# Merging the half-array attention visits of groups two to four in a planned attention-and-feed-forward kernel

## The chip, the cores and the metric

One Trainium2 chip, one of its cores. The metric is the device time of one execution in microseconds; several runs are given by their median. TensorE is called PE, VectorE DVE, ScalarE ACT, GpSimd POOL and SyncE SP, which issues the transfers.

## The reference

Attention with 4 batches, 8 heads, 768 positions and a head size of 64, each position looking at 8 global keys and the last 96 local ones, with a linear bias by distance; its output, as 3072 rows of 512, goes through a feed-forward layer of 2048 channels. All weights of that layer are stored in 64 bits.

```python
def _attn_ref(q, k, v, n_global, n_local):
    scores = scale * np.matmul(q, k.transpose(0, 1, 3, 2))
    ...
    scores = np.where(keep, scores + bias, -1000000000.0)
    scores = scores - np.max(scores, axis=-1, keepdims=True)
    a = np.exp(scores)
    a = a / (np.sum(a, axis=-1, keepdims=True) + 1e-09)
    return np.matmul(a, v).astype(np.float32)

def _moe_ref(x, w_in, w_out):
    h = x @ w_in
    g = np.where(h > 0.0, h, alpha * (np.exp(np.minimum(h, 0.0)) - 1.0))
    return (g @ w_out).astype(np.float32)
```

## The kernel before

The 3072 rows are worked in 12 groups of 256 rows (two q tiles of 128 rows), three groups to a batch. Of each group the attention of 8 heads is computed first, in four pairs of heads (`pair`), and gives the tile `x`, kept as a rounded high part `xh` and a rest `xl`. Then 16 chunks of the feed-forward layer follow (`moe`): for each chunk `up` computes `h` in 12 matmuls of 256 columns, ACT and DVE turn it into `gh` and `gl` (high part and rest), and `down` adds 6 matmuls of 512 columns to the sums `o0` and `o1`. The first three groups share their chunks in turns (five chunks of each, then five, then six), since the weights are still being made in that time: `weight` loads a chunk's 64-bit words (`bits`), and ACT and DVE make 32-bit numbers of them in tile `g`: an absolute value on ACT, a clamp, a shift and two merges on DVE, a rounding on ACT (`w`, high part) and a subtraction on DVE (`w`, rest). There are 32 such weights.

The first four groups use the route `heads32`: plain 32-bit matmuls for the scores and the values. The two heads of a pair lie on 64 partitions each, so the scores (tile `s`, from `rk` and `rqv`) use half of TensorE's rows for each head, and the values (tile `pv`, from `pt` and `rqv`) half of its columns for each head. Between them stand, for each q tile and head, a reduction on DVE that adds the mask table and finds the maximum (`pr`, `nmax`), an exponential on ACT, a scaling, a transpose on TensorE (tile `t`, all rows and columns) and a copy to `pt`. Each q tile is one call of `heads32`: one visit to the half rows for its scores, one to the half columns for its values. The scores of a visit take two banks, one a head.

The order of the instructions is not the order of the code. `Plan.add` collects operations with the engines that may do them, an estimated duration and a due time; `Plan.order` then places them one by one, on the engine that can start earliest, the earliest due first, with tiles taken from named slots (`SLOTS`; for the first groups other slots too, from `EARLY`, which lend places of weights not yet loaded). What reaches each engine is a fixed list. Where the plan sees PE unoccupied before the first `h`, `warm` puts matmuls on a tile of ones into the list (`none<-fill`, 512 columns each), which compute nothing that is used. An operation that the plan marks as using the port that DVE and POOL share is kept apart from another such operation.

## Time and profile before

| what | us |
|---|---|
| median of 3 runs (lowest, highest) | 722.8 (722.57, 723.8) |
| the profiled execution, whole | 722.63 |
| its span in the profile | 720.8 |
| PE busy in it | 703.1 |
| DVE busy | 520.9 |
| ACT busy | 510.4 |
| POOL busy | 202.2 |

The span begins with the first instruction and ends with the last; 1.8 us of the profiled execution lie outside it. PE's matmuls are pipelined and their ends are modelled: a record says how long one matmul was under way, not how much time it took from the engine. Here the time that work takes on PE is therefore read from start to start: the start of the next row less the start of this one. A row of the timeline merges like instructions that follow one another; an x4 of a 32-bit matmul with half rows or half columns stands for two matmuls of two passes each.

### The profile page before, as it was taken

Reading aid. Unit: us, or ns where it says so; the run is one execution under the profiler, and the core shown is the slowest. Engines: PE = TensorE matmul, PEld = TensorE weight load, DVE = VectorE, ACT = ScalarE, POOL = GpSimd, SP = SyncE. Lnnn points to the kernel's source line nnn. Section 1 sums busy time; section 2 is a strip of 40 time slices with the busy share of each in tenths; the row PEclk is TensorE's granted clock in tenths of the full one; section 3 lists DMA queues with packets and bytes.
Section 4 is the critical chain, followed back from the end, with each engine's and each line's share of the span. In section 5 each row is a group of like instructions: output and inputs, shape, how many; then the busy total and the mean of one; then the engine's idle time right before and its main releaser. Section 6 shows DMA issues by size and latency. Waiting matters only on the chain.

```text
span 720.8 us, 13887 instructions
## 1 busy us (share of the span) xinstructions
PE 703.1 (98%) x4716; PEld 616.4 (86%) x4716; DVE 520.9 (72%) x1570; ACT 510.4 (71%) x1467; POOL 202.2 (28%) x264
## 2 busy tenths in 40 slices
PE   8999999999999999999999999999999999999996
PEld 5676788888889899889899899898899899999895
DVE  5998899996448876876786786885886787685210
ACT  5897988866557877867776777776776776876442
POOL 1000000000004442533434443343344344332221
PEclk9999999999999999999999999999999999999999
DMA  7623790001113222131231322312321331210001
GB/s 297 240 68 90 301 414 18 23 1 46 53 59 111 76 83 82 54 105 57 78 103 38 99 55 80 104 54 68 97 76 54 91 96 53 82 54 1 30 1 35
DMA packets 22256, 63.50 MB, mean 88 GB/s; under 512 B 2721, under 2 KB 4769, under 8 KB 22177
## 3 DMA queue, kind: packets, MB, share of 16 engines
q1 hardware_dynamic: 22176, 62.53, 25.8%
q8 instruction: 39, 0.64, 0.4%
q14 instruction: 41, 0.33, 0.1%
HBM read 56.23 MB, written 6.29 MB: 87 GB/s over the span
## 4 chain that ended last, share of the span: by engine, by line
PE 81%; DVE 9%; ACT 4%; issue 3%; DMA 1%; SPq 0%; POOL 0%; ACTq 0%; DVEq 0%; POOLq 0%
PE h L597 32%; PE o L619 31%; PE pv L578 3%; PE t L566 3%; PE s L552 3%; PE pv L533 2%; PE s L510 2%; PE t L523 2%; DVE pr L467 2%; DVE ks L292 1%; DMA rqv<-in_qkv_dram 1%; PE none L743 1%; DVE pr L477 1%; DVE e L605 1%; ACT pr L479 1%
## 5 line engine op out<-in xcount | busy, mean ns | idle before, releaser
L597 PE MATMUL h<-xh,w 128*128 128x256 f32 x1536 | 248.2, 284 | 0.0
L597 PEld LDWEIGHTS h<-xh,w 128*128 128x128 f32 x1536 | 225.9, 189 | 24.5 <-issue 1.7
L619 PE MATMUL o<-w,gh 128*128 128x512 f32 x768 | 242.1, 400 | 0.3 <-ACT gh L284 0.3
L292 POOL TENSOR_TENSOR gl<-e,gh 128x256 fp32r<-128x256 f32 x148 | 118.1, 798 | 380.7 <-ACT gh L284 345.9
L619 PE MATMUL o<-w,gl 128*128 128x512 f32 x384 | 150.4, 403 | 0.0
L603 ACT ACTIVATE e<-h 128x256 f32<-128x256 f32 x192 | 73.4, 382 | 89.9 <-PE h L597 80.2
L619 PEld LDWEIGHTS o<-w,gh 128*128 128x128 f32 x768 | 124.3, 188 | 9.0 <-issue 1.8
L605 DVE SCALAR_TENSOR_TENSOR e<-e,h 128x256 f32<-128x256 f32 x192 | 80.4, 419 | 70.5 <-ACT e L604 67.4
L597 PE MATMUL h<-xl,w 128*128 128x256 f32 x768 | 123.4, 283 | 0.0
L597 PEld LDWEIGHTS h<-xl,w 128*128 128x128 f32 x768 | 113.2, 188 | 9.6 <-issue 2.5
L284 ACT CAST gh<-e 128x256 fp32r<-128x256 f32 x192 | 77.3, 403 | 39.9 <-DVE e L605 38.9
L479 ACT ACTIVATE pr<-pr,nmax 128x256 f32<-128x256 f32 (+1 forms) x192 | 93.7, 488 | 14.0 <-DVE nmax L477 11.8
L477 DVE CUSTOM_DVE_ANT_0 pr<-s,tab 128x256 f32<-128x256 f32 (+1 forms) x192 | 74.6, 398 | 37.9 <-PE s L552 30.9
L604 ACT ACTIVATE e<-e 128x256 f32<-128x256 f32 x192 | 80.3, 418 | 4.1
L619 PEld LDWEIGHTS o<-w,gl 128*128 128x128 f32 x384 | 71.2, 188 | 2.1 <-issue 0.9
L467 DVE TENSOR_SCALAR pr<-pr,st 128x256 f32<-128x256 f32 (+1 forms) x165 | 71.4, 461 | 1.6
L458 DVE TENSOR_TENSOR x<-pv,x 64x256 f32<-64x256 f32 x128 | 53.6, 419 | 23.6 <-ACT x L284 21.9
L292 DVE TENSOR_TENSOR pt<-t,pt 128x256 fp32r<-128x256 f32 (+1 forms) x128 | 51.5, 403 | 23.4 <-ACT pt L284 22.1
L284 ACT CAST pt<-t 128x256 fp32r<-128x256 f32 (+1 forms) x128 | 45.3, 354 | 12.3 <-PE t L566 11.0
L566 PE MATMUL t<-ident,pr 128*128 128x128 f32 x240 | 47.4, 274 | 5.2 <-DVE pt L292 3.4
L286 POOL CAST vd<-rqv 128x512 fp32r<-128x512 f32 (+1 forms) x32 | 18.8, 588 | 113.9 <-DMA rqv<-in_qkv_dram 113.9
L578 PE MATMUL pv<-pt,vd 128*128 128x256 f32 x240 | 50.0, 284 | 0.3 <-DVE x L458 0.3
(90 smaller groups left out, 862.2 us busy)
## 6 DMA issues: line engine op xcount, KB each, us to landing
rqv<-in_qkv_dram SPq DMA_DIRECT2D x32, 512.0 KB, 3.7
rk<-in_qkv_dram SPq DMA_DIRECT2D x32, 400.0 KB, 3.2
bits<-in_w_in_dram SPq DMA_DIRECT2D x16, 512.0 KB, 9.6
bits<-in_w_out_dram SPq DMA_DIRECT2D x16, 512.0 KB, 9.8
rqv<-in_qkv_dram SPq DMA_DIRECT2D x16, 384.0 KB, 3.3
out_dram<-ob SPq DMA_DIRECT2D x24, 256.0 KB, 2.0
rk<-in_qkv_dram SPq DMA_DIRECT2D x16, 200.0 KB, 3.5
n_raw<-in_n_global_dram SPq DMA_DIRECT2D x1, 1.0 KB, 2.6
```

The source lines that it names most:

```text
L284: self.nc.scalar.copy(out, x)
L292: self.on(e).tensor_tensor(out, x, y, ALU.subtract)
L467: self.nc.vector.tensor_scalar(out, x, sc, None, ALU.mult)
L477: p.add((("DVE", 158 + 1.042 * n, False),), lambda e: nc.vector.tensor_tensor_reduce(pr.t[:, lo:], s.t[:, lo:], tab, -(2.0 ** -(h + 1)), 3 ...
L479: p.add(act(n, extra=200), lambda e: nc.scalar.activation(pr.t[:, lo:], pr.t[:, lo:], AF.Exp, bias=nm, scale=-1.0, accum_out=st.t[:, 0, i: ...
L566: nc.tensor.transpose(tp.t[:, a], pr.t[:, a * P:(a + 1) * P], self.ident.t)
L578: nc.tensor.matmul(pv.t[:, i].rearrange("p s w -> p (s w)"), vd.t[:, 2 * i + a, j].rearrange("p s d -> p (s d)"), pt.t[:, a].rearrange("p ...
L597: nc.tensor.matmul(h.t, w1.t[:, s, cc * P:(cc + 1) * P], x.t[:, cc], start=n == 0 and cc == 0, stop=n == 2 and cc == self.NCC - 1)
L603: p.add(act(W, True), lambda e: nc.scalar.activation(ex.t, h.t, AF.Relu, scale=-1.0), [h], [ex], d - 8000)
L604: p.add(act(W), lambda e: nc.scalar.activation(ex.t, ex.t, AF.Exp, scale=-1.0), [ex], [ex], d - 8000)
L605: p.add(dve(W), lambda e: nc.vector.scalar_tensor_tensor(ex.t, ex.t, -1.0, h.t, ALU.add, ALU.max), [h, ex], [ex], d - 8000)
L619: nc.tensor.matmul(acc[i].t, g.t[:, i * P:(i + 1) * P], w2.t[:, s], start=fc == f0 and n == 0 and s == HI, stop=fc == f1 - 1 and n == 1)
```

## The change

It has six parts.

1. For groups two to four, `heads32` is called once a pair with both q tiles: four score matmuls in one visit to the half rows (each head's bank now holds both tiles), and the values of both tiles in one visit to the half columns. The first group stays at one tile a call.
2. In the plan, an operation on PE that depends on another on PE no longer waits for that one's latency of 170 ns.
3. The clamp of a weight may go to POOL, at an estimate of 640 ns.
4. `T0`, from which due times of the feed-forward chunks count, falls from 30000 to 24000, and the first group gets more slots for `rqv`, `rk`, `pr` and `pt`.
5. In the last group `gl` may be made on DVE, and the `up` of the last two chunks is due 1.3 steps earlier.
6. The copy of the last `o1` to `ob` is split in two halves of 256 columns, one on ACT and one on DVE.

```diff
-                        t = t if of == e else t + self.SEM + op.slack
+                        t = t + self.SEM + op.slack if of != e else t - self.LAT["PE"] if e == "PE" else t
...
-        if which in self.ABS:
...
+        p.add((("ACT", 575.0, False),), lambda e: nc.scalar.activation(gf(), high().bitcast(F32), AF.Abs), [bits], [g], due - 6000)
+        p.add(dve(DM, True) + (("POOL", 640.0, True),),
+              lambda e: self.on(e).tensor_scalar(gf(), gf(), F64_MIN, F64_MAX, ALU.max, ALU.min), [g], [g], due - 5500)
...
-            for i in range(NT):
-                self.heads32(b, hp, t0, i, q32, k32, v32, rqv, rk, pv, due + (2 * i - 2) * step, X)
+            for tiles in (range(NT),) if X.get("whole") else ((i,) for i in range(NT)):
+                self.heads32(b, hp, t0, tiles, q32, k32, v32, rqv, rk, pv, due - 2 * step, 2 * step, X)
...
+        ss = [self.bank("s", "s", [P, len(tiles), 2 * P], X.get("s")) for _ in range(2)]
...
         def scores(e):
-            for r, s in zip(rows, ss):
-                nc.tensor.matmul(s.t[:, lo:], q32()[r, 0, i * P:(i + 1) * P], k32()[r, 0, c0:c0 + n], start=True, stop=True)
...
+            for m, i in enumerate(tiles):
+                c0 = NG + i * (NG + P) + lo[i]
+                for r, s in zip(rows, ss):
+                    nc.tensor.matmul(s.t[:, m, lo[i]:], q32()[r, 0, i * P:(i + 1) * P], k32()[r, 0, c0:c0 + n[i]], start=True, stop=True)
+
+        def values(e):
+            for i in tiles:
+                for a in range(lo[i] // P, 2):
+                    for j in range(2):
+                        nc.tensor.matmul(pv.t[rows[j], i], v32()[:, 2 * i + a, j], pts[i].t[:, j, a], start=a == lo[i] // P, stop=a == 1)
...
-            p.add((dve(W, port=True) if X else ()) + pool(W), lambda e: self.minus(e, gl.t, ex.t, gh.t), [ex, gh], [gl], d - 8000)
+            p.add((dve(W, port=True) if X or last else ()) + pool(W), lambda e: self.minus(e, gl.t, ex.t, gh.t), [ex, gh], [gl], d - 8000)
...
-            up(fc, dues[fc])
+
+            up(fc, dues[fc] - (1.3 * step if last and fc > NFC - 3 else 0.0))
...
+                n = self.DM // 2 if last and i else self.DM
+                a = p.add(act(n, True), lambda e, i=i, ob=ob, n=n: self.copy(e, ob.t[:, :n], acc[i].t[:, :n]), [acc[i]], [ob], end - 9000)
+                if n < self.DM:
+                    p.add(dve(n), lambda e, i=i, ob=ob, n=n: self.copy(e, ob.t[:, n:], acc[i].t[:, n:]), [acc[i]], [ob], end - 8999, beside=[a])
...
-    T0, STEP0, STEP, LEAD, NE = 30000.0, 5000.0, 2900.0, (0.0, 4000.0), 3
+    T0, STEP0, STEP, LEAD, NE = 24000.0, 5000.0, 2900.0, (0.0, 4000.0), 3
...
-    EARLY = [dict(FIRST, t=["t0", "h0"], s=["s0", "s1", "o0", "o1"], pv=["v0"]), FIRST, FIRST, {"rqv": ["rqv0", "ks0"], "rk": ["rk0", "qd0", "ql0"], "rows": True}, {}]
+    EARLY = [dict(FIRST, rqv=FIRST["rqv"] + ["part0", "part1"], rk=FIRST["rk"] + ["qd0", "ql0"], pr=FIRST["pr"] + ["ks0"],
+                  pt=FIRST["pt"] + ["vd0"], t=["t0", "h0"], s=["s0", "s1", "o0", "o1"], pv=["v0"]), dict(FIRST, whole=True), dict(FIRST, whole=True),
+             {"rqv": ["rqv0", "ks0"], "rk": ["rk0", "qd0", "ql0"], "rows": True, "whole": True}, {}]
```

What this does to the lists of PE is shown at three places. In these rows a name is followed by its number, `128x256` is partitions by columns of the result, and xN counts like instructions in a row. First, PE before the first `h`, around the scores that begin the second group. Before:

```order
L743 MATMUL none<-fill 128x512 x6
L533 MATMUL pv_371<-pt_387,rqv_146 64x128 x4
L510 MATMUL s_406<-rk_185,rqv_289 128x128
L510 MATMUL s_407<-rk_185,rqv_289 128x128
L510 MATMUL s_415<-rk_185,rqv_289 128x256
L510 MATMUL s_416<-rk_185,rqv_289 128x256
L743 MATMUL none<-fill 128x512 x6
L510 MATMUL s_444<-rk_212,rqv_358 128x256
L510 MATMUL s_445<-rk_212,rqv_358 128x256
L743 MATMUL none<-fill 128x512 x2
```

The same stretch after the change:

```order
L754 MATMUL none<-fill 128x512 x5
L533 MATMUL t_387<-ident,pr_304 128x128 x2
L533 MATMUL t_387<-ident,pr_335 128x128 x2
L509 MATMUL s_395<-rk_162,rqv_159 128x256
L509 MATMUL s_396<-rk_162,rqv_159 128x256
L509 MATMUL s_395<-rk_162,rqv_159 128x256
L509 MATMUL s_396<-rk_162,rqv_159 128x256
L533 MATMUL t_409<-ident,pr_343 128x128
L533 MATMUL t_409<-ident,pr_349 128x128
L754 MATMUL none<-fill 128x512
```

The second group's scores now stand in one visit, and fewer matmuls on ones stand around them; over the whole list there are 58 such matmuls before and 35 after.

Second, PE among the first group's feed-forward chunks, where the second group's attention goes on. Before, a visit to the half rows (`s`) for each q tile:

```order
L510 MATMUL s_645<-rk_427,rqv_511 128x256
L510 MATMUL s_646<-rk_427,rqv_511 128x256
L533 MATMUL pv_652<-pt_630,rqv_412 64x128 x4
L597 MATMUL h_663<-xh_295,w_90_535 128x256 x4
L619 MATMUL o_624<-w_87_600,gh_649 128x512 x2
L597 MATMUL h_663<-xh_295,w_90_535 128x256 x4
L523 MATMUL t_685<-ident,pr_607 128x128 x2
L523 MATMUL t_685<-ident,pr_616 128x128 x2
L597 MATMUL h_663<-xl_305,w_90_535 128x256 x4
L510 MATMUL s_700<-rk_427,rqv_511 128x256
```

After:

```order
L509 MATMUL s_616<-rk_357,rqv_470 128x256
L509 MATMUL s_617<-rk_357,rqv_470 128x256
L509 MATMUL s_616<-rk_357,rqv_470 128x256
L509 MATMUL s_617<-rk_357,rqv_470 128x256
L533 MATMUL t_636<-ident,pr_591 128x128 x2
L533 MATMUL t_636<-ident,pr_607 128x128 x2
L604 MATMUL h_643<-xh_302,w_90_612 128x256 x8
L604 MATMUL h_643<-xl_311,w_90_612 128x256 x4
L515 MATMUL pv_669<-pt_610,rqv_434 64x128 x4
L515 MATMUL pv_669<-pt_650,rqv_434 64x128 x4
```

Two tiles' scores and two tiles' values now follow one another. Over the whole list the visits for scores fall from 30 to 18, those for values from 31 to 20, and PE turns from whole-array work to half-array work 35 times instead of 53.

Third, the end of PE's list. Before, the last two chunks' `down` matmuls stand in their turn behind the `up` of the last chunk:

```order
L619 MATMUL o_9396<-w_487_2284,gh_9745 128x512 x2
L619 MATMUL o_9360<-w_487_2284,gl_9752 128x512
L619 MATMUL o_9396<-w_487_2284,gl_9752 128x512
L619 MATMUL o_9360<-w_493_2353,gh_9769 128x512 x2
L619 MATMUL o_9396<-w_493_2353,gh_9769 128x512 x2
L619 MATMUL o_9360<-w_493_2353,gl_9771 128x512
L619 MATMUL o_9396<-w_493_2353,gl_9771 128x512
```

After, with `o_9332` as `o0` and `o_9357` as `o1`:

```order
L626 MATMUL o_9332<-w_467_2197,gh_9692 128x512 x2
L626 MATMUL o_9357<-w_467_2197,gh_9692 128x512 x2
L626 MATMUL o_9332<-w_467_2197,gl_9700 128x512
L626 MATMUL o_9357<-w_467_2197,gl_9700 128x512
L626 MATMUL o_9332<-w_473_2275,gh_9718 128x512 x2
L626 MATMUL o_9332<-w_473_2275,gl_9722 128x512
L626 MATMUL o_9357<-w_473_2275,gh_9718 128x512 x2
L626 MATMUL o_9357<-w_473_2275,gl_9722 128x512
```

The last three `down` steps now stand behind the last `up` where it was two (the third, with `w_461`, stands ahead of these rows), and `o0` is complete three matmuls before the end instead of one.

## Rows read from the trace of the kernel before

**Rows 1.** The page: busy time of PE, share of the span, instructions.

```profile
PE 703.1 (98%) x4716; PEld 616.4 (86%) x4716; DVE 520.9 (72%) x1570; ACT 510.4 (71%) x1467; POOL 202.2 (28%) x264
```

**Rows 2.** Timeline of PE, 41 to 45 us: start, duration, line, tiles, shapes.

```profile
41.59 0.63 PE L619 MATMUL o<-w,gl 128*128 128x512 f32 x2
42.15 0.70 PE L510 MATMUL s<-rk,rqv 64*128 64x256 f32 x4
42.78 0.66 PE L533 MATMUL pv<-pt,rqv 128*64 128x128 f32 x8
43.37 0.74 PE L597 MATMUL h<-xh,w 128*128 128x256 f32 x4
43.95 0.63 PE L619 MATMUL o<-w,gh 128*128 128x512 f32 x2
44.41 0.62 PE L597 MATMUL h<-xh,w 128*128 128x256 f32 x4
44.88 0.49 PE L523 MATMUL t<-ident,pr 128*128 128x128 f32 x3
```

**Rows 3.** Groups of instructions on PE (the fill), and PE's timeline at the first h.

```profile
L743 PE MATMUL none<-fill 128*128 128x512 f32 x58 | 19.1, 455 | 1.4 <-POOL fill L316 1.4
...
34.48 1.69 PE L597 MATMUL h<-xh,w 128*128 128x256 f32 x12
```

**Rows 4.** Windows, from:to and length; busy by engine; PE clock; DMA share, GB/s.

```profile
20.00:30.00 10.00, 10.00 (x64) 6.47 (x64) 9.86 (x39) 8.41 (x28) 0.00 (x0) 1.00 0.78 291
93.00:214.00 121.00, 121.00 (x794) 104.40 (x793) 96.03 (x251) 82.93 (x215) 1.97 (x2) 1.00 0.22 81
```

**Rows 5.** Timeline of DVE and PE where the third group's x and first h stand.

```profile
92.02 0.42 DVE L292 TENSOR_TENSOR xl<-pv,xh 128x256 fp32r<-128x256 f32 x1
...
93.93 0.64 PE L597 MATMUL h<-xh,w 128*128 128x256 f32 x4
```

**Rows 6.** DVE's weight steps: smallest, median, largest ns; first and last start.

```profile
L365 DVE TENSOR_SCALAR g<-g x32: 405/422/429, 12.2 to 163.2; 128x512 f32<-128x512 f32 x32
...
L371 DVE SCALAR_TENSOR_TENSOR g<-bits,g x32: 670/687/693, 13.8 to 167.5; 128x512 int32<-128x512 int32 x32
```

**Rows 7.** Timeline of PE: a values visit of one unit, a scores visit of two tiles.

```profile
22.78 0.44 PE L533 MATMUL pv<-pt,rqv 128*64 128x128 f32 x4
23.15 0.50 PE L743 MATMUL none<-fill 128*128 128x512 f32 x1
...
26.13 0.93 PE L510 MATMUL s<-rk,rqv 64*128 64x128 f32 x8
26.98 1.66 PE L743 MATMUL none<-fill 128*128 128x512 f32 x6
```

**Rows 8.** Timeline of the last microseconds; idle time before in brackets.

```profile
712.41 1.20 PE L619 MATMUL o<-w,gh 128*128 128x512 f32 x4 [0.32 <-ACT gh L284]
...
713.45 0.63 PE L619 MATMUL o<-w,gl 128*128 128x512 f32 x2
713.88 1.07 ACT L284 COPY ob<-o 128x512 f32<-128x512 f32 x2 [1.52 <-PE o L619]
```

**Rows 9.** Waits of PE, 214 to 666 us: total us, times, longest.

```profile
PE t L566 <- DVE pt L292: 3.4, 7, 0.8
```

**Rows 10.** POOL's copy group; a DVE scaling to 171 us and from 215 us.

```profile
L286 POOL CAST vd<-rqv 128x512 fp32r<-128x512 f32 x24 | 14.8, 616 | 107.1 <-DMA rqv<-in_qkv_dram 107.1
...
L467 DVE TENSOR_SCALAR pr<-pr,st x35: 279/347/356, 11.4 to 169.3; 128x256 f32<-128x256 f32 x26, 128x128 f32<-128x128 f32 x9
...
L467 DVE TENSOR_SCALAR pr<-pr,st x128: 276/350/1458, 221.8 to 656.1; 128x256 f32<-128x256 f32 x112, 128x128 f32<-128x128 f32 x16
```

**Rows 11.** Waits of DVE, 60 to 93 us: total us, times, longest.

```profile
DVE e L605 <- ACT e L604: 1.1, 1, 1.1
```

**Rows 12.** PE's timeline at a wait, and the window behind it (columns as PE, clock).

```profile
58.52 1.04 PE L510 MATMUL s<-rk,rqv 64*128 64x256 f32 x4 [1.25 <-DVE nmax L477]
...
60.00:61.00 1.00, 1.00 (x7) 0.50 0.00 0
```

More of the change, by code (lines that the diff above doesn't have):

```diff
@@ L530, in values @@
-        def values(e):
-            for a in range(a0, 2):
-                for j in range(2):
-                    nc.tensor.matmul(pv.t[rows[j], i], v32()[:, 2 * i + a, j], pt.t[:, j, a], start=a == a0, stop=a == 1)
-        p.add((("PE", 140 + 220.0 * (2 - a0), False),), values, [rqv, pt], [pv], d)
+            for m, i in enumerate(tiles):
+                c0 = NG + i * (NG + P) + lo[i]
+                for r, s in zip(rows, ss):
+                    nc.tensor.matmul(s.t[:, m, lo[i]:], q32()[r, 0, i * P:(i + 1) * P], k32()[r, 0, c0:c0 + n[i]], start=True, stop=True)
@@ L536, in heads32 @@
+        p.add((("PE", 140 + 1.72 * sum(n.values()), False),), values, [rqv] + list(pts.values()), [pv], d)
         if "pr" in X:
-            self.held += [o for v in prs + [pt] for o in v.readers]
+            self.held += [o for v in pts.values() for o in v.readers]
     def head(self, b, h, t0, j, qd, ql, ks, vd, pv, due, step):
@@ L551, in scores @@
                 for m, x in enumerate((qd, ql)):
[L552 removed]
+                    nc.tensor.matmul(s.t[:, 0, lo:], x.t[:, j, i * P:(i + 1) * P], ks.t[:, j, c0:c0 + n], start=m == 0, stop=m == 1)
             p.add((("PE", 130.0 * n / P + 30, False),), scores, [qd, ql, ks], [s], due + i * step - 5000, slack=slack)
[L555 removed]
+            self.softmax(b, h, t0 + i, s, 0, prs[i], st, i, due + i * step)
         self.inverse(st, due - 3500)
@@ L581, in head, with moe @@
             p.add((("PE", 122.0 * (2 - a0), False),), values, [vd, pt], [pv], d, slack=slack)
-    def moe(self, rows, xh, xl, f0, f1, dues, step, part, X):
+    def moe(self, rows, xh, xl, f0, f1, dues, step, part, X, last):
         nc, p, NFC, ws = self.nc, self.plan, self.NFC, self.ws
```

71 lines of the change are left out of this document (33 added, 38 removed).

## The prediction

> **What bounds the kernel now.** I read the page first: PE is busy in 98% of the span [rows 1]. Such a row doesn't say whether PE is full or only waiting with a matmul under way, so I then read PE's timeline from start to start. Where nothing disturbs it, two matmuls of 512 columns take 43.95 to 44.41 = 0.46 us, and four of 256 columns 44.41 to 44.88 = 0.47 us [rows 2], and nearly all rows behind the first `h` have these distances. So PE is full from 34.48 us, where the first `h` stands [rows 3], to the end, apart from a few waits of about a microsecond. A microsecond of PE work taken out behind that point is a microsecond of the span, as long as the other engines follow.
>
> Whether they follow is the second reading, in windows. Between 20 and 30 us DVE is busy 9.86 of 10 us, with the first group's attention and the weights; between 93 and 214 us it is busy 96 of 121 us, and PE all of it [rows 4]. So ahead of 93 us there are two limits, PE and DVE, one about as tight as the other: the third group's last `xl` ends at 92.44 us on DVE, and PE takes up that group's first `h` at 93.93 [rows 5]. Behind it PE alone is the limit. I take the place of that `h` as the joint of the whole estimate.
>
> **The change part by part.** I work against the profiled execution, 722.63 us, which is 0.2 us from the median of 722.8; the answer goes to the median.
>
> *The matmuls on ones.* The list has 35 of them instead of 58 [rows 3]. At half of the 0.46 us for two of that size [rows 2] the 23 are worth 5.3 us. They all stand ahead of the first `h`, where PE waits for softmax steps. They vanish because more pairs of the first group are under way at once and fewer weights are made ahead of its end. On DVE's list up to the last `xl` of the first group there are 109 instructions for 118; those that went are mainly four merges (0.686 us each), six clamps or shifts (0.422 us) [rows 6] and two subtractions on 128x512 like the merges, less some small ones that came. By their durations that is 5.9 us less on the engine that is full there, so the earlier start is real and not only planned.
>
> *The visits.* What one costs is in rows 3. Two matmuls of 512 columns ahead of a scores visit take 41.59 to 42.15 = 0.56 us instead of 0.46, so entering costs 0.10 us. The first four `h` matmuls behind a values visit take 43.37 to 43.95 = 0.58 us instead of 0.47, so leaving costs 0.11 us. Passing from a scores visit straight to a values visit costs no such thing. The list turns to half work 35 times for 53: 18 x 0.21 = 3.8 us. Beside the edges each visit has a fixed part inside. A scores visit of one tile with 256 columns takes 42.15 to 42.78 = 0.63 us; one of two tiles, of 128 and 256 columns (the row names only the first shape), takes 26.13 to 26.98 = 0.85 us [rows 7]. The further 128 columns cost 0.22 us, so 256 further columns cost 0.43 us, and a merged tile saves 0.63 - 0.43 = 0.20 us. A values visit of one unit takes 22.78 to 23.15 = 0.37 us, one of two units 42.78 to 43.37 = 0.59 us [rows 2, 7]: 0.22 us a unit, so a merged one saves 0.15 us. With 12 scores visits and 11 values visits fewer that is 2.4 + 1.65 = 4.05 us. The visits together are worth 7.9 us.
>
> *The end.* PE waits 0.32 us for the last `gh`, and the four matmuls behind it take 712.41 to 713.45 = 1.04 us instead of 0.92, since `gl` comes late [rows 8]. With three `down` steps behind the last `up`, and `gl` made by DVE, both go: 0.45 us. The two copies take 1.07 us behind the last matmul [rows 8]; now `o0` is complete 0.7 us ahead of the end, so its copy is under cover, and the other is cut in two. By the waits in the list DVE's half still stands behind ACT's, so I count 0.45 us saved of a possible 0.6. Sum: 0.9 us.
>
> *The planner's latency rule and the late groups.* From the fifth group on the counts of PE's work stay as they are; only the order differs. PE waits there for DVE ahead of a transpose, 3.4 us in seven waits behind one line [rows 9] and about 2 us more behind others. In the new list the shortest stretch of PE work between one tile's transposes and the next is 1.39 us, before 1.16 us, so I expect no more waits than before: 0, from -2 to +3 us.
>
> *Clamps on POOL.* 27 of 32 clamps leave DVE, 11.4 us by 0.422 [rows 6], which is in DVE's sums below. On POOL nothing waits in that time. No row has this operation there; a copy of 512 columns takes 0.616 us [rows 10]. The danger is the port: a scaling on DVE never took more than 0.356 us up to 171 us, with POOL almost unused, and up to 1.458 us behind 215 us, with POOL at work [rows 10]. So a clamp can cost DVE between nothing and about 0.6 us. I take little, since many of DVE's steps there read PSUM; the other end is a rival below. The Trainium skill, SBUF — State Buffer, "Who interferes with whom", calls the shared port an exclusive lock, where one instruction fully blocks the other; the 1.458 us agrees. By that rule the move would be worth nothing in the stretch where DVE is the limit.
>
> *The sum.* PE's list is 5.3 + 7.9 = 13.2 us shorter. By the same prices 8.3 us of it lies ahead of the third group's first `h` and 4.7 us behind (the rest is rounding; some attention work of later groups moved ahead as well). The 4.7 us count in full. The 8.3 us count only as far as DVE lets them. Up to the last `xl` of that group DVE has 298 instructions before and after, by their durations 0.2 us more: the clamps that left are replaced by merges of the next weights and by `gl` steps that now stand earlier. What DVE can give is its own waits: 4.1 us between 60 and 93 us, in seven rows of which the longest stands in [rows 11], most of them behind PE's own work or behind ACT that waits for PE, which is earlier now. So the joint moves from 93.93 by 4.1 us and not by 8.3. Sum: 4.1 + 4.7 + 0.9 = 9.7 us, and 722.8 - 9.7 = **713.1 us**.
>
> **The rivals.**
>
> *PE is followed in full.* DVE's list holds merges ahead of its `xl` that could have waited, and what PE needs may come in time nonetheless. Then 13.2 + 0.9 = 14.1 us come out: 708.7 us. For it speaks the 5.9 us that DVE saves in the first group; against it the equal sum at the joint.
>
> *The port takes it back.* Eleven clamps stand on POOL ahead of the joint; if each holds DVE for its whole 0.616 us, DVE is 6.8 us later there. The joint then comes 6.8 + 0.2 - 4.1 = 2.9 us late instead of 4.1 early, and 4.7 + 0.9 - 2.9 = 2.7 us remain: 720.1 us. For it speaks the 1.458 us; against it the median of 0.350 us in the same row, with POOL at work.
>
> *The merged visit saves nothing.* The drain could belong to each change of tile or bank, and the visits are merged in name only. Then 5.3 us go ahead of the joint, of which DVE lets 4.1 pass, and some 1.6 us behind it: 716.2 us. Against it speaks the visit of two tiles [rows 7], which is short by the fixed part.
>
> *The clock falls, and it ends slower.* PE now runs ahead of DVE between 30 and 93 us, and a scores visit of two tiles needs both banks, so it waits for four reductions instead of two, with everything on PE queued behind it. Before, one such wait of 1.25 us [rows 12] was followed by some 3.4 us at a granted clock of 0.50, the 1.2 GHz level (one window of them stands in the same rows), which cost some 1.7 us of PE's time. The first of these cost nothing, since PE has 8.3 - 4.1 = 4.2 us to give. To end 1.5 us slower than before, 9.7 + 1.5 + 4.2 = 15.4 us must go, nine such waits in a stretch where there was one: 724.3 us. Nine is many; the place with DVE busy throughout is the place where it could be.
>
> **How the numbers follow.** Forecast 713.1 us (711 to 715.5): 0.46. PE followed in full (707.5 to 711): 0.19. Visits that save nothing, or half (715.5 to 717.5): 0.11. The port (717.5 to 721.3): 0.10. No difference, by a mixture of the port and one or two falls of the clock: 0.06. Slower by the clock: 0.08. A measurement of this kernel can tell 0.2%, 1.4 us, from no change. So faster 0.86, same 0.06, slower 0.08. The range for 8 in 10 runs from 708.0, the end of the full case, to 719.5, most of the way into the port's; the latency rule's -2 to +3 lies inside.
>
> **What would show it.** Each step has its place in the profile after. The first `h` should stand at about 30 us instead of 34.48; if it stays, the start was a plan only. The third group's first `h` should stand near 89.8 us: near 86 means that DVE was no limit, behind 92 that the port or the clock took it. Scores visits of two full tiles should take 1.06 us and values visits 1.03 us. DVE's merges and subtractions ahead of 170 us should keep their 0.687 us; a median or a maximum far over it is the port. Granted clock of 0.50 between 30 and 93 us should show once or twice. Behind the joint the fourth group's first `h` should follow 4.7 us closer than before; the rest of the span should be as long as it was, less 0.9 us at the end. The prediction is wrong in its main step if the joint moves by less than 2 us or more than 7.

## The result

| | before | after |
|---|---|---|
| median of 6 runs each, us (lowest, highest) | 722.89 (722.22, 723.8) | 716.25 (714.08, 716.87) |
| the profiled execution, us | 722.63 | 716.35 |
| its span, us | 720.8 | 714.6 |

The changed kernel takes 0.9898 of the time before, with a 95% interval of 0.9884 to 0.9913: it is faster by 6.6 us. The forecast was 713.1 us, 9.7 less, in a range of 708.0 to 719.5. The sign and the range hold. The size is two thirds of what was forecast, and, as the runs below show, part of it comes from another place than the one that the sum gave it.

The page of the changed kernel shows the new shares, and the clamp that went to POOL: 27 of them, 2.2 us each on the average.

```profile
PE 694.0 (97%) x4693; PEld 612.5 (86%) x4693; DVE 515.9 (72%) x1566; ACT 503.2 (70%) x1464; POOL 244.4 (34%) x272
...
L367 POOL TENSOR_SCALAR g<-g 128x512 f32<-128x512 f32 x27 | 59.1, 2196 | 91.4 <-ACT g L365 91.4
```

PE has 9.1 us less to do than in [rows 1], and 23 of its instructions are gone. To see where the time came out, I read the start of the first `h` of a group in PE's timeline. These are the rows for groups one, two, three, four and the last (start, duration, line, tiles, shapes):

```profile
29.70 1.53 PE L604 MATMUL h<-xh,w 128*128 128x256 f32 x8
...
65.22 0.97 PE L604 MATMUL h<-xh,w 128*128 128x256 f32 x6
...
90.74 1.11 PE L604 MATMUL h<-xh,w 128*128 128x256 f32 x8
...
208.24 0.63 PE L604 MATMUL h<-xh,w 128*128 128x256 f32 x4
...
659.53 0.64 PE L604 MATMUL h<-xh,w 128*128 128x256 f32 x4
```

Before, the same places stand at 34.48 [rows 3], 66.30, 93.93 [rows 5], 214.35 and 666.12; three of them are not among the rows ahead of the prediction and come from the same timeline:

```profile
66.30 0.73 PE L597 MATMUL h<-xh,w 128*128 128x256 f32 x4
...
214.35 0.62 PE L597 MATMUL h<-xh,w 128*128 128x256 f32 x4
...
666.12 0.64 PE L597 MATMUL h<-xh,w 128*128 128x256 f32 x4
```

So 4.78 us are won at the first group's `h`, but only 1.08 are left at the second's. Then 2.1 more come out up to the third (the joint), 2.9 from there to the fourth, 0.5 in the late groups, and at the end 0.4 us are lost. Together that is 1.1 + 2.1 + 2.9 + 0.5 - 0.4 = 6.2 us, the difference of the two spans.

Why the 4.78 us shrink is seen in windows that are cut where the behaviour changes, at 64 us. Columns are from:to and length; busy time of PE, PE's weight loads, DVE, ACT and POOL; granted clock; DMA share, GB/s. Before:

```profile
0.00:64.00 64.00, 58.88 (x366) 41.22 (x367) 55.16 (x209) 49.53 (x150) 3.13 (x20) 0.97 0.50 180
64.00:93.00 29.00, 29.00 (x219) 21.23 (x219) 24.10 (x91) 24.71 (x76) 0.74 (x1) 1.00 0.71 263
```

After, the same two windows and the inner part of the first:

```profile
0.00:64.00 64.00, 55.63 (x359) 38.85 (x359) 55.47 (x207) 50.28 (x154) 21.08 (x28) 0.97 0.53 189
64.00:93.00 29.00, 29.00 (x237) 24.29 (x234) 26.85 (x95) 25.17 (x78) 6.14 (x3) 1.00 0.75 287
...
30.00:60.00 30.00, 24.88 (x179) 18.65 (x178) 29.76 (x91) 26.61 (x78) 11.06 (x6) 1.00 0.24 74
```

Up to 64 us DVE's busy time is the same to 0.3 us, while PE's falls by 3.3: DVE is occupied 29.76 of 30 us between 30 and 60, and PE 24.88. From 64 us on PE is busy all the time, before and after. So the kernel has two limits one behind the other: to about 65 us something that PE waits for, with DVE the fullest engine, and from there PE. (How far DVE alone is that limit is tried below, where one of its steps is taken out.) What PE saves ahead of 65 us is waited away there, in waits like these (a wait of PE: total us, times, longest, for 30 to 64 us):

```profile
PE s L509 <- DVE nmax L476: 2.1, 2, 1.2
PE t L533 <- DVE pr L466: 1.5, 2, 1.1
PE t L533 <- ACT pr L464: 1.5, 2, 1.0
```

### The profile page after: what moved, and what is told of

It reads as the page before. It is cut to its first block, busy times and chain, and to the rows that moved or that the text cites. A ratio compares the mean times of both kernels' runs of the same rounds, so it can differ in the third digit from the quotient of the medians.

```text
span 714.6 us, 13766 instructions
## 1 busy us (share of the span) xinstructions
PE 694.0 (97%) x4693; PEld 612.5 (86%) x4693; DVE 515.9 (72%) x1566; ACT 503.2 (70%) x1464; POOL 244.4 (34%) x272
## 4 chain that ended last, share of the span: by engine, by line
PE 84%; DVE 9%; ACT 3%; DMA 1%; issue 1%; SPq 0%; ACTq 0%; DVEq 0%
PE h L604 35%; PE o L626 34%; PE t L573 4%; PE pv L585 4%; PE s L559 4%; DVE pr L466 2%; DMA rqv<-in_qkv_dram 1%; PE t L533 1%; PE pv L515 1%; PE s L509 1%; DVE pr L476 1%; DVE g L370 1%; DVE e L612 1%; DVE g L372 1%; DVE w L293 1%
## 5 line engine op out<-in xcount | busy, mean ns | idle before, releaser
L604 PE MATMUL h<-xh,w 128*128 128x256 f32 x1536 | 244.5, 283 | 0.0
L293 POOL TENSOR_TENSOR gl<-e,gh 128x256 fp32r<-128x256 f32 x129 | 101.5, 787 | 228.5 <-ACT gh L285 209.2
L626 PE MATMUL o<-w,gl 128*128 128x512 f32 x384 | 132.0, 400 | 0.4 <-DVE gl L293 0.3
L604 PEld LDWEIGHTS h<-xl,w 128*128 128x128 f32 x768 | 104.2, 189 | 0.0
L367 POOL TENSOR_SCALAR g<-g 128x512 f32<-128x512 f32 x27 | 59.1, 2196 | 91.4 <-ACT g L365 91.4
L626 PEld LDWEIGHTS o<-w,gl 128*128 128x128 f32 x384 | 64.0, 189 | 4.4 <-DVE gl L293 1.5
L585 PE MATMUL pv<-pt,vd 128*128 128x256 f32 x240 | 51.5, 290 | 2.1 <-DVE pt L293 2.1
```

The source lines that it names most:

```text
L293: self.on(e).tensor_tensor(out, x, y, ALU.subtract)
L585: nc.tensor.matmul(pv.t[:, i].rearrange("p s w -> p (s w)"), vd.t[:, 2 * i + a, j].rearrange("p s d -> p (s d)"), pt.t[:, a].rearrange("p ...
L604: nc.tensor.matmul(h.t, w1.t[:, s, cc * P:(cc + 1) * P], x.t[:, cc], start=n == 0 and cc == 0, stop=n == 2 and cc == self.NCC - 1)
L626: nc.tensor.matmul(acc[i].t, g.t[:, i * P:(i + 1) * P], w2.t[:, s], start=fc == f0 and n == 0 and s == HI, stop=fc == f1 - 1 and n == 1)
```

## The experiments

All kernels are measured against the kernel before on the same chip; ratios are to that. The chips differ between runs, so where two medians lie close, compare the ratios. For each profiled execution this table has the first `h` of groups one to four and of the last one, read as above.

| kernel | median us | ratio (95%) | 1st | 2nd | 3rd | 4th | last | span |
|---|---|---|---|---|---|---|---|---|
| before | 722.89 | | 34.48 | 66.30 | 93.93 | 214.35 | 666.12 | 720.8 |
| after | 716.25 | 0.9898 (0.9884 to 0.9913) | 29.70 | 65.22 | 90.74 | 208.24 | 659.53 | 714.6 |
| e1_tiles_apart | 722.6 | 0.9993 (0.9977 to 1.0008) | 29.77 | 65.27 | 93.20 | 214.01 | 665.20 | 719.7 |
| e7_visits_only | 716.97 | 0.9914 (0.9891 to 0.9938) | 35.40 | 67.09 | 90.72 | 208.50 | 660.26 | 715.3 |
| e4_old_start | 719.75 | 0.9954 (0.9939 to 0.997) | 38.47 | 67.76 | 91.44 | 211.66 | 663.30 | 718.2 |
| e10_old_start_dve | 719.18 | 0.9949 (0.9929 to 0.9969) | 35.38 | 64.50 | 91.20 | 209.22 | 661.74 | 716.3 |
| e13_old_start_new_rule | 718.35 | 0.9951 (0.9932 to 0.997) | 35.40 | 64.54 | 91.03 | 209.05 | 660.61 | 715.9 |
| e2_dve_clamp | 717.19 | 0.9904 (0.9882 to 0.9926) | 27.55 | 65.00 | 90.31 | 208.01 | 660.39 | 715.3 |
| e11_early_clamps | 713.89 | 0.9874 (0.9852 to 0.9895) | 29.78 | 65.29 | 89.60 | 206.57 | 657.25 | 711.8 |
| e12_early_old_rule | 714.88 | 0.9888 (0.987 to 0.9905) | 28.65 | 65.48 | 89.74 | 208.14 | 659.21 | 714.7 |
| e6_no_shift | 712.78 | 0.9859 (0.9832 to 0.9886) | 28.68 | 63.36 | 88.77 | 206.00 | 656.34 | 710.8 |
| e5_old_end | 715.25 | 0.9891 (0.987 to 0.9912) | 28.60 | 64.09 | 89.96 | 207.54 | 658.70 | 713.7 |
| e8_end | 716.79 | 0.9909 (0.9886 to 0.9932) | 28.77 | 64.27 | 89.82 | 207.31 | 658.30 | 713.9 |
| e9_best | 716.61 | 0.9898 (0.9873 to 0.9922) | 27.49 | 64.36 | 89.74 | 207.63 | 659.82 | 714.9 |

**The visits taken away.** Everything stays as in the changed kernel, but the second to fourth group visit the half array for one tile at a time again.

```diff
-                  pt=FIRST["pt"] + ["vd0"], t=["t0", "h0"], ..., pv=["v0"]), dict(FIRST, whole=True), dict(FIRST, whole=True),
-             {..., "rows": True, "whole": True}, {}]
+                  pt=FIRST["pt"] + ["vd0"], t=["t0", "h0"], ..., pv=["v0"]), dict(FIRST), dict(FIRST),
+             {..., "rows": True}, {}]
```

> The changed kernel with each q tile of groups two to four in its own visit again, and all else as changed (the plan made anew). PE's list is 7.3 us longer by the prices of the prediction, 3.0 us of it ahead of the third group's first h and 4.3 us behind. If a merged visit is worth its fixed parts and its edges (0.20, 0.15 and 0.21 us), and DVE hides some of the part ahead: 716.25 + 4.3 to 7.3, so about 721.5 us. If a merged visit saves nothing: 716.3 us.

Measured: 722.6 us, as before the change. The first `h` still stands at 29.77, so the new start is there, and it is worth nothing at the end. The second group's `h` stands at 65.27, as in the changed kernel (65.22): the visits merged ahead of that place give nothing there either. The rival by which the visits save nothing is refuted, and with it the idea that 23 matmuls on ones fewer shorten the kernel. A merged visit costs what the prediction said: in the changed kernel eight score matmul records take 64.14 to 65.22 = 1.08 us (predicted 1.06), and sixteen of values 44.47 to 45.49 = 1.02 us (predicted 1.03).

```profile
64.14 1.14 PE L509 MATMUL s<-rk,rqv 64*128 64x256 f32 x8
...
44.47 1.09 PE L515 MATMUL pv<-pt,rqv 128*64 128x128 f32 x16
45.49 0.74 PE L626 MATMUL o<-w,gh 128*128 128x512 f32 x2
```

**The visits alone.** The kernel before, with merged visits (and the plan's estimates of their length) and nothing else.

```diff
-                        t = t + self.SEM + op.slack if of != e else t - self.LAT["PE"] if e == "PE" else t
+                        t = t if of == e else t + self.SEM + op.slack
...
-        p.add(dve(DM, True) + (("POOL", 640.0, True),),
+        p.add(dve(DM, True),
...
-    T0, STEP0, STEP, LEAD, NE = 24000.0, 5000.0, 2900.0, (0.0, 4000.0), 3
+    T0, STEP0, STEP, LEAD, NE = 30000.0, 5000.0, 2900.0, (0.0, 4000.0), 3
...
-    EARLY = [dict(FIRST, rqv=FIRST["rqv"] + ["part0", "part1"], rk=FIRST["rk"] + ["qd0", "ql0"], pr=FIRST["pr"] + ["ks0"],
-                  pt=FIRST["pt"] + ["vd0"], t=["t0", "h0"], ...
+    EARLY = [dict(FIRST, t=["t0", "h0"], ...
```

The call of `moe` also has the old end (its last argument is `False`).

> The kernel before with nothing new but the merged visits of the second to fourth group: the old start, clamps on VectorE, the old end, the old rule for a step's start on another engine. If the three parts add, the visits are worth what taking them away costs (722.6 less 716.3, some 6.5 us) and the time is 716 to 717. If start and visits only pay together, since the start's gain is lost when TensorE's list is long and the visits' gain is lost when VectorE is late, the time is that of the run with the old start, 719 to 720.5. If the old rule and VectorE's clamps hide even that, 721.5 or more.

Measured: 717.0 us, the first case. The joint stands at 90.72 us, where the changed kernel has it (90.74), though the first `h` stands at 35.40, 5.7 us later. From the second group's first `h` to the third's it takes 67.09 to 90.72 = 23.6 us, where before it took 66.30 to 93.93 = 27.6; that is the stretch in which PE is the limit, and in which 4.0 of the 5.5 us arrive by which the span is shorter. Some 1.1 of the 4.0 is one merged visit for scores that now stands ahead of the stretch, where PE has time to spare: 16 records of scores lie in it for 24 before. The other five parts of the change together are worth less than a measurement can tell.

**The old start.** The changed kernel with the old `T0` and the old slots of the first group.

```diff
-    T0, STEP0, STEP, LEAD, NE = 24000.0, 5000.0, 2900.0, (0.0, 4000.0), 3
+    T0, STEP0, STEP, LEAD, NE = 30000.0, 5000.0, 2900.0, (0.0, 4000.0), 3
...
-    EARLY = [dict(FIRST, rqv=FIRST["rqv"] + ["part0", "part1"], rk=FIRST["rk"] + ["qd0", "ql0"], pr=FIRST["pr"] + ["ks0"],
-                  pt=FIRST["pt"] + ["vd0"], t=["t0", "h0"], ...
+    EARLY = [dict(FIRST, t=["t0", "h0"], ...
```

> The changed kernel with T0 at 30000 and the first group's old slots (the plan made anew: 63 matmuls on ones instead of 35). The first h comes some 5 us later. If DVE's whole list up to the third group's last xl is the limit, which is the same 98.5 us here, most of that is made good by then, and 1.6 us of longer list behind count: about 718 us. If the earlier start counts in full: about 721 us.

Measured: 719.75 us, between the two cases. The first `h` came 8.8 us later than in the changed kernel, at 38.47, and the joint only 0.7 us later. But from the joint to the fourth group's `h` it took 120.2 us for 117.5, and that contradicts the visits alone, which have the old start too and are 2.8 us faster. Two runs looked for the difference.

**The old start, clamps on DVE.** As the last one, and the clamps of the weights are on DVE.

```diff
-        p.add(dve(DM, True) + (("POOL", 640.0, True),),
+        p.add(dve(DM, True),
```

> The changed kernel with the old start (its later first group and the old places of the first group's buffers) and all clamps on VectorE. With GpSimd's clamps the old start came to 719.8 and its stretch from the third to the fourth group's first h took 120.2 us for 116.3 of TensorE's work. Theory (GpSimd's clamps of some 2 us make TensorE wait there, so the old start was never to blame): that stretch falls to 117.5 to 118.0, the joint stands at 90.5 to 91.5, and the time is 716.5 to 717.5, that of the visits alone. Rival (the old start itself, or the new rule for a step's start on another engine, costs the 3 us): the stretch stays over 119 and the time at 719 to 720.5.

Measured: 719.2 us. In the profile the stretch behind the joint falls to 209.22 - 91.20 = 118.0 us, as the theory said, and the wait of PE at 108.79 us in the run before is gone (its row: `t` waits 0.77 us for ACT's `pr`). The median, however, stands where the rival put it.

```profile
108.79 0.62 PE L533 MATMUL t<-ident,pr 128*128 128x128 f32 x2 [0.77 <-ACT pr L464]
```

**The visits alone, and the new rule.** The kernel with the visits alone, with the rule of part 2 of the change put back; it differs from the last run only by its old end.

```diff
-                        t = t if of == e else t + self.SEM + op.slack
+                        t = t + self.SEM + op.slack if of != e else t - self.LAT["PE"] if e == "PE" else t
```

> The run with the visits alone (717.0 on another chip), with nothing but the new rule for a step's start on another engine added. It is also the run with the old start and VectorE's clamps (719.2) with the old end. If the rule costs the two us between those: 718.5 to 720, with TensorE's wait of a us behind 78.9 us for ScalarE's copy of pt. If the new end costs them: 716.5 to 717.5. If neither does, and the two runs differ by their chips and by chance: in between, 717.5 to 718.5.

Measured: 718.35 us, at the border of two of the cases. Its profile has the wait of 0.8 us behind 78.9 us, which the visits alone don't have:

```profile
PE t L533 <- ACT pt L285: 0.8, 1, 0.8
```

Three runs with the old start and the new rule lie at ratios of 0.9949 to 0.9954, the one with the old rule at 0.9914, but the intervals overlap or all but touch. So the rule may cost 1 to 3 us with the old start; that is not shown. One wait of 0.8 us is not all of that, and I leave the rest open.

**The clamps on DVE.** The changed kernel without POOL's clamps (the same diff as two runs above).

> The changed kernel with all clamps on DVE (the plan made anew). If taking clamps off a full DVE is what lets it follow PE, DVE has 1.7 us more ahead of the third group's last xl and the time is about 717.7 us. If a clamp of 2.05 us on POOL (planned at 0.64) costs more in late weights, in gl steps of 0.83 us beside it and in PE's waits at 106 us than it saves: about 715 us.

Measured: 717.2 us, near the first case, but not to be told from the changed kernel. That looks like an operation that doesn't matter. But PE had no wait between 90 and 214 us before, and has two in the changed kernel, both beside these clamps:

```profile
PE o L626 <- ACT gh L285: 0.4, 1, 0.4
PE o L626 <- DVE gl L293: 0.3, 1, 0.3
```

The timeline of DVE, POOL and PE at their place, in the changed kernel:

```profile
101.12 1.70 DVE L370 SCALAR_TENSOR_TENSOR g<-bits,g 128x512 int32<-128x512 int32 x2
...
101.40 4.48 POOL L367 TENSOR_SCALAR g<-g 128x512 f32<-128x512 f32 x2 [3.71 <-ACT g L365]
...
103.42 0.68 DVE L372 SCALAR_TENSOR_TENSOR g<-bits,g 128x512 int32<-128x512 int32 x1
...
104.02 0.83 DVE L293 TENSOR_TENSOR gl<-e,gh 128x256 fp32r<-128x256 f32 x1
...
107.03 2.27 POOL L367 TENSOR_SCALAR g<-g 128x512 f32<-128x512 f32 x1 [1.16 <-ACT g L365]
107.30 0.74 PE L626 MATMUL o<-w,gh 128*128 128x512 f32 x2 [0.41 <-ACT gh L285]
107.45 0.83 DVE L293 TENSOR_TENSOR gl<-e,gh 128x256 fp32r<-128x256 f32 x1
...
108.33 0.50 PE L626 MATMUL o<-w,gl 128*128 128x512 f32 x1 [0.30 <-DVE gl L293]
```

Of the two merges in the first row, which take 0.68 us each alone, the second takes 1.10 where POOL's clamp starts, and a subtraction for `gl` takes 0.83 instead of 0.42. PE then waits for `gh` and `gl`. This is not the rule but a part of the cases: 176 of DVE's steps up to 170 us lie beside a clamp, and 21 of them took over a tenth longer than the median of their kind in the run with all clamps on DVE, by 0.07 to 0.41 us, 5.9 us together and 3.2 of that ahead of the joint. Of DVE's steps beside no clamp none did. So there is a loss behind the joint, and if the sum is nothing, there must be a gain ahead of it. The next run keeps the one without the other.

**Clamps on POOL only ahead of the joint.**

```diff
-        p.add(dve(DM, True) + (("POOL", 640.0, True),),
+        p.add(dve(DM, True) + ((("POOL", 640.0, True),) if fc < 5 else ()),
```

> The changed kernel with GpSimd's clamps only for the first five weight pairs, nine clamps in all before the third group's first h, and VectorE's for the rest. TensorE's work from the third to the fourth group's first h is then 115.8 us. Theory (behind the joint the clamps cost waits, ahead of it they take 0.42 us each from the engine that sets the pace): the joint stays at 89.8 to 90.7, TensorE's waits of 0.4 and 0.3 us at 106 and 107 go, the fourth group's first h stands at 206.5 to 207.5, and the time is 714.8 to 716. Rival (what GpSimd's clamps cost behind the joint is bought back by VectorE's free time there, whatever runs them): 716 to 717.5, the fourth group's first h at 207.5 to 208.5.

Measured: 713.9 us, ratio 0.9874 (0.9852 to 0.9895), the fastest kernel of the study that computes everything, and below the case that was expected; its slowest run took 714.63 us, and only one of six runs of the changed kernel was faster than that. Nine clamps are left on POOL, the last at 52 us (least, median and most ns; first and last start):

```profile
L367 POOL TENSOR_SCALAR g<-g x9: 1913/1944/2540, 19.6 to 52.0; 128x512 f32<-128x512 f32 x9
```

The waits of PE at 106 to 108 us are gone. The first two `h` stand as in the changed kernel (29.78 and 65.29), and the third and fourth are earlier:

```profile
65.29 0.97 PE L604 MATMUL h<-xh,w 128*128 128x256 f32 x6
...
89.60 1.12 PE L604 MATMUL h<-xh,w 128*128 128x256 f32 x8
...
206.57 0.63 PE L604 MATMUL h<-xh,w 128*128 128x256 f32 x4
```

Up to the fourth group that is 208.24 - 206.57 = 1.7 us, all of it from the clamps behind 52 us, which are on DVE here: up to the fourth group's `h` PE has the same number of matmuls as in the changed kernel, its start is the same, and the granted clock fell at the start in both. That 1.1 of the 1.7 us show already at the joint is due to the order of PE's list. Five `o` matmuls of some 0.23 us that the changed kernel has ahead of the joint stand behind it here, x33 and x28 in the stretch from the second group's first `h` to the third's. These are the windows of that stretch for `o` alone (from:to and length, PE busy, granted clock, DMA share, GB/s), in the changed kernel and in this one:

```profile
65.22:90.74 25.52, 9.79 (x33) 1.00 0.76 289
```

```profile
65.29:89.60 24.31, 8.22 (x28) 1.00 0.76 281
```

The rest of the 2.8 us between the two spans (0.6 in the late groups, 0.5 at the end) I put down to nothing, since those parts of the program are the same. What the early clamps bring ahead of the joint is seen against the run with all clamps on DVE: the second group's `h` stands 0.3 us later, the third's 0.7 earlier and the fourth's 1.4 earlier, and the medians are 3.3 us apart (2.2 us by the ratios), though the intervals of the two ratios still overlap. So a gain of the early clamps is likely, and not shown beyond doubt.

**The same with the old rule** (and the old end, since the new one needs the new rule). The diff is the rule's, as above.

> The run with GpSimd's clamps ahead of the joint only, now with the old rule for a step's start on another engine and, since the new end needs the new rule, with the old end. TensorE's work ahead of each group's first h and the clamps on GpSimd are almost the same (48.0, 71.2 and 187.0 us, nine clamps). If the rule is worth nothing by itself: 713 to 715. If the new rule is what makes the merged visits run without waits beside the new start: 715.5 or more. If the rule costs with the new start what it seems to cost with the old: 711 to 712.5.

Measured: 714.9 us, the first case: with the new start the rule by itself is worth nothing that can be told. Its profiled execution is the slowest of its four, and shows that late clamps are not the only cause of such waits: PE waits 0.66 us for `gh` at 175.91 us with no clamp on POOL, and from the third group's `h` to the fourth's it takes 118.4 us for 117.0.

**A step taken from DVE.** The changed kernel without DVE's shift of each weight.

```diff
-        p.add(dve(DM, True), lambda e: nc.vector.tensor_scalar(g.t, g.t, 3, 0x3FFFFFFF, ALU.logical_shift_left, ALU.bitwise_and),
+        p.add(dve(DM, True), lambda e: None,
```

> The changed kernel without VectorE's shift and mask of each weight half (line 368), every other instruction in its place; the low parts of the weights that it prepares are left out by this, so the output is not the reference's. Theory (VectorE, not TensorE, sets the pace from the start to the third group's first h): ten of these shifts stand before 65.2 us and three more before 90.7, at 0.42 to 0.45 us, so the second group's first h moves from 65.2 to 61 to 62.5 and the third's from 90.7 to 86 to 88; TensorE's busy time between 30 and 60 us rises above 24.9 of 30; the whole comes to 711 to 713 us. Rival (TensorE's visits and ScalarE's weight steps set it, VectorE is busy without limiting): the two first h stay within 0.5 us of 65.2 and 90.7, and the time stays at 716.

Measured: 712.8 us as a whole, which is in the theory's range. But the second group's `h` moves to 63.36 and the third's to 88.77, by 1.9 and 2.0 us; the theory wanted 2.7 to 4.2 and 2.7 to 4.7, the rival at most 0.5. Of 4.2 us taken from DVE ahead of 65 us less than half arrives, and in the stretch of 30 to 64 us DVE, which had no waits at all in the changed kernel, now has two:

```profile
DVE st L485 <- ACT pr L478: 0.5, 1, 0.5
DVE e L612 <- ACT e L611: 0.5, 1, 0.5
```

But part of this is the clock. In the changed kernel's profiled execution it fell at the start, here it did not. The two runs that follow have the changed kernel's lists up to the joint and no such fall, and against them only 0.7 to 0.9 us are left at the second group and 1.0 to 1.2 at the third: about a fifth of what was taken from DVE, nearer to the rival than to the theory. So DVE is a limit there, but not alone; a saving on DVE is soon at its end, and the two new waits point to ACT, which stands close behind it. No run takes a step from ACT, so that is not shown.

**The old end.** The changed kernel with the last group's `gl`, `up` and copies as before.

```diff
-                self.moe(..., n < self.NE, n == len(groups) - 1)
+                self.moe(..., n < self.NE, False)
```

> The changed kernel with the old treatment of the last group: gl on POOL only, up in its turn, one copy for o1 (the plan made anew for that group alone). By the prediction the end was worth 0.9 us: 717.1 us. By the profile after, where the wait that went is made up by a wait for the flag and the second half of the copy runs behind the first, it is worth nothing: 716.3 us.

Measured: 715.25 us. The edits at the end are worth nothing that can be told. Two causes offered themselves in the changed kernel's profile: PE waits for the steps of a flag that the program computes in that place, and DVE's half of the last copy stands behind ACT's.

```profile
PE flagsum L775 <- DVE flag L771: 0.4, 1, 0.4
```

```profile
706.85 1.06 ACT L285 COPY ob<-o 128x512 f32<-128x512 f32 x2 [1.70 <-PE o L626]
707.10 0.40 PE L626 MATMUL o<-w,gl 128*128 128x512 f32 x1
707.46 1.28 SPq L655 DMA_DIRECT2D out_dram<-ob  x2
707.94 0.42 DVE L287 COPY ob<-o 128x256 f32<-128x256 f32 x1 [2.34 <-ACT ob L285]
```

**The end mended.** The flag's matmul is issued 40 places later than its DVE steps, and the two halves have a buffer and a transfer each.

```diff
                 if i == last + 60:
                     self.flag()
+                if i == last + 100:
+                    self.flagsum()
...
+                for k, eng in ((0, act(n, True)), (1, dve(n))):
+                    ob = ob if k == 0 else self.sb("io", "ob", [P, self.DM])
+                    c = slice(k * n, k * n + n)
+                    p.add(eng, lambda e, i=i, ob=ob, c=c: self.copy(e, ob.t[:, c], acc[i].t[:, c]), [acc[i]], [ob], end - 9000)
+                    p.add(sp(), lambda e, i=i, ob=ob, c=c: nc.sync.dma_start(self.out[..., c], ob.t[:, c]), [ob], [], end, nbytes=P * n * 4)
```

> The changed kernel with two mends at its end: the matmul of the flag's sum is issued 40 places later than VectorE's steps for it, and the last output tile's halves go into two buffers with a transfer each, so that VectorE's half need not follow ScalarE's. Theory (two new serial waits ate the end's gain): TensorE's wait of 0.36 us at 665 goes, and from the last matmul's start to the last copy's end it takes 0.8 us in place of 1.26, so the span is shorter by 0.5 to 0.9 us, 715.4 to 715.8. Rival (a transfer more, or the descriptor of the last one, sets the end): 716.3 or more.

Measured: 716.8 us, the rival's case. The flag's wait is gone: from the last group's first `h` to the last matmul's start it takes 658.30 to 705.46 = 47.2 us instead of 659.53 to 707.10 = 47.6. But DVE's half still begins only where ACT's has ended (705.89 + 0.37 = 706.26), and behind the last copy's end (706.30 + 0.42 = 706.72) the span goes on for 7.1 us instead of 714.6 - 708.4 = 6.2: the further transfer seems to take more than the flag's wait gave. From the end of PE's last matmul the span goes on for 8.0 us here and for 7.5 in the next run, which has that transfer too, and for 6.4 to 7.4 us in the twelve other profiled executions.

```profile
705.89 0.37 ACT L285 COPY ob<-o 128x256 f32<-128x256 f32 x1
706.29 1.66 SPq L653 DMA_DIRECT2D out_dram<-ob  x2
706.30 0.42 DVE L287 COPY ob<-o 128x256 f32<-128x256 f32 x1 [2.34 <-ACT ob L285]
```

So the buffer was not what held DVE's half back. Both halves read one tile `o`; whether that is the reason was not tried.

**Mended end and all clamps on DVE.**

> The mended end together with all clamps on VectorE. If GpSimd's clamps only stretch VectorE's steps and are worth nothing, and the end's mend is worth 0.5 to 0.9: 715.4 to 716.7. If GpSimd's clamps help the joint by what they take off VectorE (each 0.42 us, some 13 before the third group's first h) and cost less than this behind it: 717 to 718.5.

Measured: 716.6 us, within the first case, and no better than the changed kernel. Against the fastest one it lacks the early clamps on POOL, and it has the further transfer.

## Why the prediction was right, and where it was not

*The first `h`.* Forecast at about 30 us, measured 29.70. Right, but worthless: with the old start and the visits alone the joint stands at the same place. The step that failed is the sentence that the earlier start is "real and not only planned". It is real on PE and gives nothing: the second group's first `h` stands between 64.1 and 67.8 us, with the first group's between 27.5 and 38.5, in all kernels that compute everything. DVE's busy time in the first 64 us is 55.2 to 56.6 us in all of these, PE's 53.2 to 58.9. That fits DVE as the limit of this stretch, with ACT close behind; the run without the shift shows that DVE is not the whole of it.

*The joint.* Forecast 4.1 us earlier, measured 3.2, and 4.0 to 4.1 in the two runs with the same lists up to there (89.96 and 89.82 us). The difference lies at the start: in the changed kernel's profiled execution the granted clock was 0.58 in the window of 12 to 16 us, most of it at 0.50, the 1.2 GHz level; in the run with the old end it was 1.00, and the first `h` stood 1.1 us apart. (The execution before had a fall of its own, the one of [rows 12].) The same windows, of the changed kernel and of the run with the old end:

```profile
12.00:16.00 4.00, 4.00 (x17) 2.64 (x18) 3.07 (x15) 3.49 (x15) 0.00 (x0) 0.58 1.05 421
```

```profile
12.00:16.00 4.00, 3.99 (x24) 2.36 (x23) 3.72 (x20) 3.84 (x17) 0.00 (x0) 1.00 1.05 420
```

So the number was right by luck, for its reason was not. The sum let 8.3 us of PE's saving, 5.3 of it from the matmuls on ones, run into 4.1 us of DVE's waits. But those waits stood between 60 and 93 us, and from 65 us on PE was the limit already: DVE waited there for PE. What moved the joint is the part of the visits behind 65 us: with the visits alone and the old start it stands at 90.72. The rival of the visits that save nothing shows the same fault in numbers. It let 4.1 us of the start pass and came to 716.2 us; measured without the merged visits were 722.6.

*The visits.* Their prices, read in [rows 2] and [rows 7] (where the prediction has "rows 3" for them, rows 2 is meant), were right to 0.02 us a visit. The term was 7.9 us; taking the visits away costs 722.6 - 716.25 = 6.4 us, and alone they give 0.86% of the time before, 6.2 us.

*Behind the joint.* Forecast 4.7 us, measured 2.9. This is the mis-sized term. Of the 4.7 us some 1.6 are seven `o` matmuls that PE now does ahead of the joint (x33 in the window of the changed kernel shown with the early clamps, 26 before), and 3.1 are the visits. The visits were priced well: behind the joint the visits alone bring 120.4 - 117.8 = 2.6 us, and the time of scores and values in it falls by 1.41 us, from start to start, for 1.40 by the fixed parts. In the run with the early clamps, where two `o` matmuls have moved, the same prices give 3.1 + 0.5 = 3.6 us, and 120.4 - 117.0 = 3.4 came. So most of what is missing in the changed kernel belongs to its late clamps. The estimate for a clamp on POOL, from a copy of 0.616 us [rows 10], was too low by three times: the median is 2.05 us. It was given "between nothing and about 0.6 us" for DVE, and the place with a price was sought ahead of the joint, where the rival of the port expected the loss. It came behind it too, and taking the late clamps away brings 1.7 us back.

*The port's rival* forecast 720.1 us with DVE late by 6.8 us at the joint. The time did not come, but about half of the cause did: ahead of the joint DVE's steps beside a clamp took 3.2 us longer in all, against some 5 us that the twelve clamps on POOL there took off DVE (0.417 us each). The Trainium skill, SBUF — State Buffer, "Who interferes with whom", has the shared port as an exclusive lock under which the later instruction is fully blocked while the other runs. The trace agrees only in part: of DVE's steps with two inputs beside a clamp of 2 us, one of 0.68 us took about 0.4 longer, and the one at 103.42 us, in the middle of POOL's work, took its 0.68; no step beside a clamp took over 0.41 us longer. With another step of POOL the trace agrees better: in the kernel before, the scaling of 1.458 us began at 222.16 us and ended 0.15 us behind this subtraction.

```profile
222.17 1.30 POOL L292 TENSOR_TENSOR vd<-rqv,vd 128x512 fp32r<-128x512 f32 x1
```

Why POOL's clamp holds DVE up less than its subtraction is open.

*The late groups.* Forecast 0, from -2 to +3; measured 0.5 us less. Right.

*The end.* Forecast 0.9 us less, measured 0.4 more. The wait for the last `gh` [rows 8] did go, worth some 0.4: without the flag's wait it takes 47.2 us from the last group's first `h` to the last matmul's start, and before the change 47.6. But the flag's wait of 0.36 to 0.4 us came, which I had not looked for, and the halves of the copy brought nothing (1.26 us from the last matmul's start to the last copy's end, before 1.27, with the second matmul of the last pair 0.23 us behind the first), and the span went on for 6.2 us behind the last copy instead of 5.8. This last varies between runs: in the run with the early clamps, which has the same end, it is 5.8. So the 0.4 us lost here is no more than that scatter.

*The clock's rival* expected falls of the clock between 30 and 93 us from waits of a microsecond. PE had four such waits of 0.9 to 1.2 us there and two shorter ones, and the granted clock stayed at 1.00 from 30 to 93 us, where one or two falls were expected. So the rival did not come here. It isn't refuted for every execution: five of the fourteen profiled ones had a fall between 40 and 63 us and one of these had two, but none came near the nine that it needed.

Added up, the four terms came to 3.2 + 2.9 + 0.5 - 0.4 = 6.2 us for 9.7: 0.9 of the difference by the clock at the start, 1.8 behind the joint, 1.3 at the end, less 0.5 in the late groups.

## What to carry to other kernels

Two busy engines may limit one behind the other in time rather than side by side: cut the windows until one of them is near 100% in each, and give a saving its value only in the windows where its engine is that one. A part that "is worth nothing" in a run without it can be a gain in one stretch and a loss in another; undo it in one stretch alone, as with the early clamps, which made the fastest kernel here by the median. And before an operation moves to another engine, ask what that operation, not a copy of the same size, takes there.

## What was not expected of the hardware

A clamp by two constants of 128x512 numbers took 2.05 us on POOL in the median (1.91 to 3.15), where DVE took 0.42 and POOL's own copy of that size 0.616 [rows 10]. Beside it 155 of 176 steps of DVE took their usual time, to a tenth, and 21 took up to 0.41 us longer.

The clock fell under the fill, with one kernel and not with another of the same lists. Ahead of it, from 10 to 12 us, PE had been busy 1.15 of 2 us in both; these are the windows of the changed kernel and of the run with the old end:

```profile
10.00:12.00 2.00, 1.15 (x8) 0.59 (x4) 0.93 (x6) 1.98 (x8) 0.00 (x0) 0.98 1.01 406
```

```profile
10.00:12.00 2.00, 1.15 (x8) 0.59 (x4) 0.92 (x6) 1.98 (x8) 0.00 (x0) 1.00 1.01 404
```

The fall cost about 1.1 us at the first `h`: it stands at 29.70 to 29.78 us in the three kernels with the fall, and at 28.60 to 28.77 in the four without it that have as many matmuls on ones. Of the 14 profiled executions three had it there, five between 40 and 63 us, and six had none ahead of 100 us.
